# Bank pairs for the seven products, earlier weight sums, closer inverse units and longer first weight rows in a fused spectral-filter and gated-MLP kernel

## Chip, cores and metric

The kernel runs on one core of one Trainium2 chip. The metric is the device time in microseconds (us) of one execution; the median over several executions is compared.

## What is computed

```python
xn = layernorm(x)                        # x: (1, 2048, 512) bf16
X  = rfft2(xn, axes=(-2, -1))            # (1, 2048, 257) complex
y  = irfft2(X * (w_r + 1j * w_i), s=(2048, 512)).astype(bf16)
h  = gelu(xn @ w_gate) * (xn @ w_up)     # w_gate, w_up: (512, 1792)
out = x + y + h @ w_down                 # w_down: (1792, 512)
```

Two branches read the same normalised x: a spectral filter (a two-dimensional Fourier transform, a product with a weight per frequency, the transform back) and a gated MLP. Their results are added to x.

## The kernel before, in words

**Rows and blocks.** x lies in SBUF as `x_sb`, 16 tiles of 128 rows by 512; tile j is also where the result of these rows is summed up, and it is written out when all its parts are in. The MLP takes four tiles at a time: block b has the tiles 4b to 4b+3. `xnT` holds the normalised rows transposed.

**The MLP.** For each block and each of 14 chunks fc of 128 hidden columns, `gate` (line 842) and `up` (856) make four matmuls of 128x512 each into one PSUM bank. ScalarE takes gelu of the gate's bank into one of three `gl` buffers (854), and VectorE multiplies it with up's bank into `hT` (872). The down projection of two tiles, `down` (879), is 14 plain matmuls per tile. That of the other fourteen tiles is done two tiles at a time as seven products of half-size blocks in place of eight (`product`, 728): step 0 to 6 of product (b, p) makes seven 128x256 matmuls each, for the tiles jA = 4b+p and jB = jA+2. Some products need sums of blocks of w_down (`sums_T`, 717: T[0] to T[3], made once) and of h (`sum_01`, 692, and `sums_S`, 674). A product holds two PSUM banks, bx and by, over its seven steps: the steps use bx, bx, by, by, bx, by, by; after step 0 ScalarE copies bx to by (776), and after step 3 by to bx. VectorE adds finished parts to x_sb (`add_to`, 650) or stores them with x in `tw` (`base`, 778, for jA after step 2 and jB after step 3). From there until `release` (762), which comes for jB at step 5 and for jA at step 6, the tile is locked.

**The spectral branch.** It is cut into small units that are placed between the matmuls of the MLP. `butter` (419) folds xnT into `fold`; unit D (433) transforms along the columns, `units_A` (462) makes the first half of the transform along the rows, the result goes through DRAM (scr1) and comes back as `tv` (`load_tv`, 457). Unit B(g) and unit C(g), g = 0 to 7 (565, 588), make the second half and the first half of the transform back. Each takes two neighbouring banks, which ScalarE empties in one copy of 128x1024. Between B and C VectorE multiplies with the frequency weights (584), which are loaded in parts into a ring (`load_W`, 551; `keep_256`, 560, copies one column aside on POOL). C reads `cm`, a table loaded in four parts on POOL's queue. C's results go through DRAM (scr2) and come back as `vv` (612). The inverse units E(j) and F(j), j = 0 to 15 (618, 802), finish tile j: E is four matmuls, a ScalarE copy and a small POOL copy; F is four matmuls, a ScalarE copy and four VectorE additions (825 to 828), which leave the result in one of four `ys` buffers. `add_y` (831) then adds ys to x_sb[j] with an accumulating DMA on POOL's queue. If the tile is locked, it is put off until the release.
`mini` (491) does the same work for one left-over column.

**The order of the work.** Nothing is scheduled at run time. The Python program walks through the blocks and chunks, and `hook` (913) is called after each gate, each up and each product step (and three times in a down); it counts up, and before counting it emits whatever `at(h, ...)` has planned for this number. In the blocks 2 and 3 a turn is therefore three hooks: gate, up, product step. Block 2 starts at hook 69, block 3 at 111, product (2,0) comes just before the hooks 113, 116, ... 131, product (2,1) before 134, 137, ... 152, and the last two products (3,0) and (3,1) close the kernel with 14 steps. F(j)'s additions come right after F(j), and its add_y three hooks later. Every engine runs its own instructions in the order in which they were emitted; `op` (150) adds the semaphore waits, per tile key.

**PSUM banks.** `take(n, dur, ...)` (324) picks banks at build time by an estimate: it keeps a time pt of the work emitted so far and for each of the eight banks a time at which it should be free, and takes the n neighbouring banks whose latest time is the earliest. A product sets its banks to 1e9 until its last step.

**SBUF places.** `arena` has 8192 columns: the table `am` (0 to 3071), fold 0 (4096 to 6143) and fold 1 (6144 to 8191). T[0] to T[3], 1792 columns each, and a sum for products (0,p) use the same columns later. The last readers of fold 0 and fold 1 are the units D of tiles 8 to 11 (hooks 31 to 34) and 12 to 15 (hooks 39 to 42), that of am is units_A at hook 44. `cm` shares its columns with `ev1` and `xn`.

**Loads at the start.** SP's queue and ScalarE's queue each load one half (64 rows) of x tiles 0 and 1, then two chunks of a weight (w_up on SP, w_gate on ScalarE), the half of tiles 2 and 3, and two more chunks (352 to 357). A chunk is 128 columns, so that two chunks are rows of 512 bytes. SP's queue loads all that follows. The first six chunks of gate and up are first done for tiles 0 and 1 alone (1005 to 1023).

Of the kernel before, what the change touches and what calls it, by code (L numbers as in the profile page):

```python
# [214 lines left out]
def bass_parallel_sum__spectral_gfnet__glu_gated_geglu__prompt_kernel(  # L215
# [23 lines left out]
    wgv = B_w_gate.rearrange("(dc p) f -> p dc f", p=P)  # L239
    wuv = B_w_up.rearrange("(dc p) f -> p dc f", p=P)  # L240
    wdv = B_w_down.rearrange("(fc p) d -> p fc d", p=P)

    with ExitStack() as es:
        def sb(name, shape, dt):
            return es.enter_context(nc.sbuf_tensor(name, shape, dt))
# [6 lines left out]
        arena = sb("arena", [P, 8192], F16)  # L252
        am = arena[:, 0:3072].rearrange("p (j c) -> p j c", j=NJ)
        fold = [arena[:, 4096 + 2048 * i:6144 + 2048 * i].rearrange("p (a c) -> p a c", a=4) for i in range(2)]
        T = [arena[:, 1792 * k:1792 * k + 1792].rearrange("p (f c) -> p f c", f=7) for k in range(4)]
        AKEYS = ["am"] + [("fold", i, a) for i in range(2) for a in range(4)]
        wg_sb = sb("wg", [P, 4, FF], BF16)
        wu_sb = sb("wu", [P, 4, FF], BF16)
# [65 lines left out]
        def take(n, dur, hold=None, ops=1):  # L324
            i = min(range(9 - n), key=lambda i: max(free[i:i + n]))
            pt[0] += dur
            if hold is None:
                act_t[0] = max(act_t[0], pt[0] + 0.25) + 0.2 + 0.43 * n
                end = act_t[0]
            else:  # L330
                end = pt[0] + hold
            for k in range(i, i + n):
                free[k] = end
            return i

        def dma(eng, dst, src, r=(), w=()):
            return op(eng, lambda e: e.dma_start(dst, src), r=r, w=w, dma=True)  # L337
# [4 lines left out]
        def load_x(j0, n, b, eng):  # L342
            dma(eng, x_sb[64 * b:64 * b + 64, j0:j0 + n, :], xv[b, :, j0:j0 + n, :], w=[("x", j, b) for j in range(j0, j0 + n)])

        def load_w(t, v, nm, lo, hi, eng):
            cs = slice(P * lo, P * hi)
            dma(eng, t[:, :, cs], v[:, :, cs], w=[(nm, i) for i in range(lo, hi)])
# [4 lines left out]
        for b, eng, t, v, nm in ((0, "sp", wu_sb, wuv, "wu"), (1, "act", wg_sb, wgv, "wg")):  # L352
            load_x(0, 1, b, eng)
            load_x(1, 1, b, eng)
            load_w(t, v, nm, 0, 2, eng)
            load_x(2, 2, b, eng)
            load_w(t, v, nm, 2, 4, eng)
        op("act", lambda e: e.activation(warm_o[:], mhalf[:, 0:1], ACT.Gelu_apprx_tanh), r=["mhalf"], w=["warm_o"])
        load_w(wg_sb, wgv, "wg", 4, 6, "sp")
        load_w(wu_sb, wuv, "wu", 4, 6, "sp")  # L360
        load_x(4, 4, 0, "sp")
        load_x(4, 4, 1, "sp")
        dma("sp", fd[:], c_fd.ap(), w=["fd"])
# [243 lines left out]
        def readers(keys):  # L607
            return [ev for key in keys for ev in pr.readers.get(key, [])]
# [62 lines left out]
        def s_keys(b, k, f0, f1):  # L671
            return [("S", b, k, f) for f in range(f0, f1)]
# [35 lines left out]
        def s01(k, f0, f1):  # L708
            if k == 0:
                v = arena[:, 7168 + P * f0:7168 + P * f1]  # L710
            else:
                assert f1 <= 4 or f0 >= 4
                row = 2 * (k == 2) + (f0 >= 4)
                v = xb[:, 2048 * row + P * (f0 % 4):2048 * row + P * (f0 % 4) + P * (f1 - f0)]
            return v.rearrange("p (f c) -> p f c", c=P)

        def sums_T(k):
            B = lambda i, c: wd_sb[:, 7 * i:7 * i + 7, 256 * c:256 * c + 256]
            a, b2, r = ((B(0, 1), B(0, 0), []), (B(1, 1), T[0], [("T", 0)]), (B(1, 1), B(0, 1), []), (B(1, 0), T[1], [("T", 1)]))[k]
            op("dve", lambda e: e.tensor_tensor(T[k], a, b2, ALU.subtract), r=r + [("wd", fc) for fc in range(NFC)],  # L720
               w=[("T", k)], after=readers(AKEYS))

        wb = {}

# [3 lines left out]
        def product(b, p, step):  # L728

            jA, jB = 4 * b + p, 4 * b + p + 2  # L730
            cA, cB = slice(P * p, P * p + P), slice(256 + P * p, 256 + P * p + P)
            h = hT[b % 2]
            if step == 0:
                wb[p] = take(1, 0.0, 1e9), take(1, 0.0, 1e9)
            bx, by = wb[p]
            bk = (bx, bx, by, by, bx, by, by)[step]
            c0, c1 = slice(0, 256), slice(256, 512)
            if b < 2:
                SS = lambda k: (lambda f: s01(k, f, f + 1)[:, 0, :], [("s01", k)])
                for k in ((0, 1), (2,), (), (), (), (), ())[step]:  # L740
                    sum_01(b, p, k)
            else:
                SS = lambda k: (lambda f: ssum(b, k, f, f + 1)[:, 0, cA], s_keys(b, k, 0, 7))
            HH = lambda o, cs, t: (lambda f: h[:, f + o, cs], [("hT", b % 2, f + o, p + 2 * t) for f in range(7)])
            TT = lambda k: (lambda f: T[k][:, f, :], [("T", k)])
            BB = lambda o, cs: (lambda f: wd_sb[:, f + o, cs], [("wd", f + o) for f in range(7)])
            (st_, r1), (mv, r2) = ((HH(0, cA, 0), BB(0, c0)), (HH(7, cA, 0), BB(7, c0)), (SS(1), TT(1)), (SS(2), TT(2)),
                                   (HH(7, cB, 1), TT(3)), (SS(0), TT(0)), (SS(3), BB(7, c1)))[step]
            o = bank(bk)[:, 0:256]

            def fn(e):
                ins = None
                for f in range(7):
                    ins = e.matmul(o, st_(f), mv(f), start=(f == 0 and step in (0, 5)), stop=(f == 6), skip_group_check=True)  # L754
                return ins
            pt[0] += 0.77
            op("pe", fn, r=r1 + r2, w=[("ps", bk)])
            rk = [("ps", bk)]
            t12, t22 = tw[:, p, 0:256], tw[:, p, 256:512]
            last = b == 3  # L760

            def release(j):
                for f in locked.pop(j):
                    f()
                if last:
                    assert done[j] == 1
                    for bb, eng in ((0, "sp"), (1, "act")):
                        dma(eng, ov[bb, :, j, :], x_sb[64 * bb:64 * bb + 64, j, :], r=acc(j), w=[("out", j, bb)])
                else:
                    part_done(j)  # L770

            if b < 2 and step == 2:
                sum_01(b, p, 3)

            def copy(dst, src):
                return op("act", lambda e: e.activation(bank(dst)[:, 0:256], bank(src)[:, 0:256], ACT.Copy), r=[("ps", src)], w=[("ps", dst)], after=war(("ps", dst)))  # L776

            def base(t, j, *after):
                locked[j] = []
                op("dve", lambda e: e.tensor_tensor(t, o, x_sb[:, j, 256:512], ALU.add), r=rk + [("acc", j, 1), ("x", j, 0), ("x", j, 1)], w=[("tw", p, j == jA)],  # L780
                   after=war(("tw", p, j == jA)) + list(after))

            if step == 0:
                copy(by, bx)
            elif step == 1:
                add_to(jA, o, rk, 0)
            elif step == 2:
                base(t12, jA)
            elif step == 3:
                base(t22, jB, copy(bx, by))  # L790
            elif step == 4:
                add_to(jB, o, rk, 0)
            elif step == 5:
                add_to(jB, o, rk + [("tw", p, False)], 1, t22)
                release(jB)
            else:
                add_to(jA, o, rk + [("tw", p, True)], 1, t12)
                release(jA)
                free[bx] = free[by] = pt[0] + 1.2
            hook()  # L800
# [105 lines left out]
        def at(h, *calls):  # L906
            plan.setdefault(int(h), []).extend(calls)
# [19 lines left out]
                at(h0 + i // 2, t)  # L927
            at(89 + s // 2 if s > 3 else 47 + s, (keep_256, s))
        cmv = c_cm.ap().rearrange("p (h r c) -> p h r c", h=NJ, r=2)
        for i, h0 in enumerate((52, 57, 63, 68)):  # L930
            hs = slice(4 * i, 4 * i + 4)
            at(h0, (load_late, cm[:, hs], cmv[:, hs], [("cm", 2 * i), ("cm", 2 * i + 1)], (["ev1"], ["ev1", ("xn", 0)], [("xn", 1), ("xn", 2)], [("xn", 2), ("xn", 3)])[i]))
        at(60, (load_late, gm[:], c_g.ap().rearrange("p (a c) -> p a c", a=4), ["gm"]))
        for m in range(1, 4):
            a = (5, 15, 23)[m - 1]
            t = (16, 25, 33)[m - 1]
# [31 lines left out]
        for jg in range(4):  # L968
            at(99, (load_vv, jg))
        for j in range(NJ):  # L970
            at(107 + 2.6 * j, (unit_E, j))
            at(110.5 + 2.6 * j, (unit_F, j))
        for k in range(4):
            at(46 + k, (sums_T, k))
        for k in range(4):
            at((101, 101, 102, 103)[k], (sums_S, 2, 0, 4, (k,)))
            at((106, 106, 107, 107)[k], (sums_S, 2, 4, 6, (k,)))
# [122 lines left out]
```

## Time and profile before

| | |
|---|---|
| median of 5 runs | 187.98 us (186.61 to 191.28) |
| profiled execution, its own time | 186.61 us |
| its span (first to last instruction) | 184.8 us |
| granted TensorE clock | 1.00 in the whole span |
| gate and up matmuls (lines 851, 866), busy | 58.6 us each |
| DMA moved | 26.83 MB, 145 GB/s on average |

PE is TensorE's matmuls, PEld its weight loads, DVE VectorE, ACT ScalarE, POOL GpSimd, SP the engine that only issues DMAs. L754 is line 754 of the kernel. Matmuls are pipelined and their ends are modelled, so a busy PE is not PE at its peak. A line of waits gives the waiting instruction, what released it, the sum, how often and the longest. The chain of waits is followed back from the last instruction of the program.

### The profile page before, as it was taken

How to read it: one execution, taken by the hardware profiler on the slowest of the kernel's cores; microseconds unless marked ns; L12 is line 12 of the kernel's file. 1: busy time of each engine (PE TensorE's matmuls, PEld its weight loads, DVE VectorE, ACT ScalarE, POOL GpSimd, SP SyncE). 2: the span in 40 equal slices, each digit the busy share in tenths (PEclk: the TensorE clock that was granted, in tenths of full speed). 3: DMA queues.
4: the chain of work that ended last, by engine and by line, in shares of the span. 5: the costliest groups of instructions: out<-in, count | busy, mean ns of one | idle time of the engine just before them, and what ended most of it. 6: DMA issues, size and time to landing. Idle time of an engine off the chain costs nothing.

```text
span 184.8 us, 3814 instructions
## 1 busy us (share of the span) xinstructions
PE 175.8 (95%) x1417; PEld 107.9 (58%) x1417; DVE 130.6 (71%) x322; ACT 94.3 (51%) x157; POOL 53.8 (29%) x106
## 2 busy tenths in 40 slices
PE   7899999999999999989997999999999999899993
PEld 2478654555555454545653656556666676566882
DVE  3677899996442399647795468787875776689752
ACT  1344548676475442456664556435756766554110
POOL 2110263642316010356481000001334434434100
PEclk9999999999999999999999999999999999999999
DMA  4999998798989968255863112185145555344304
GB/s 115 285 255 311 335 278 301 201 175 173 181 134 207 120 147 121 70 167 136 220 177 88 57 57 60 58 242 216 28 82 100 103 105 109 63 73 67 79 0 114
DMA packets 27954, 26.83 MB, mean 145 GB/s; under 512 B 2992, under 2 KB 24880, under 8 KB 27808
## 3 DMA queue, kind: packets, MB, share of 16 engines
q1 hardware_dynamic: 21504, 18.04, 40.3%
q0 software_dynamic: 4272, 7.24, 18.8%
q10 hardware_dynamic: 2160, 1.31, 2.6%
q8 instruction: 11, 0.18, 0.4%
q14 instruction: 7, 0.06, 0.1%
HBM read 18.19 MB, written 6.29 MB: 132 GB/s over the span
## 4 chain that ended last, share of the span: by engine, by line
PE 69%; DVE 13%; DMA 6%; ACT 3%; issue 3%; SPq 2%; ACTq 1%; POOL 1%; DVEq 0%
PE ps L851 19%; PE ps L754 19%; PE ps L866 18%; DMA wu<-in_B_w_up_dram 4%; PE ps L887 3%; DVE hT L872 3%; DVE st L383 3%; SPq L337 2%; DMA x_sb<-tv 2%; PE ps L598 2%; DVE arena L720 2%; PE ps L626 2%; PE ps L809 2%; PE ps L573 1%; PE ps L405 1%
## 5 line engine op out<-in xcount | busy, mean ns | idle before, releaser
L851 PE MATMUL ps<-xnT,wg 128*128 128x512 f16 (+1 forms) x248 | 58.6, 359 | 0.6 <-ACT xnT L995 0.6
L866 PE MATMUL ps<-xnT,wu 128*128 128x512 f16 (+1 forms) x248 | 58.6, 359 | 0.2 <-DMA wu<-in_B_w_up_dram 0.2
L872 DVE TENSOR_TENSOR hT<-ps,gl 128x512 bf16<-128x512 f32 (+1 forms) x62 | 39.3, 636 | 20.3 <-PE ps L866 13.5
L854 ACT ACTIVATE gl<-ps 128x512 bf16<-128x512 f32 (+1 forms) x62 | 34.5, 556 | 32.3 <-PE ps L851 31.0
L866 PEld LDWEIGHTS ps<-xnT,wu 128*128 128x128 bf16 x248 | 23.4, 98 | 20.4 <-DMA wu<-in_B_w_up_dram 0.5
L851 PEld LDWEIGHTS ps<-xnT,wg 128*128 128x128 bf16 x248 | 22.9, 98 | 16.6 <-issue 2.1
L340 POOL DMA_DIRECT2D wring<-in_A_w_r_dram x32 | 18.5, 610 | 17.6 <-DVE early L584 7.5
L635 POOL COPY tv<-tv 1x128 bf16<-1x128 bf16 x16 | 4.7, 292 | 48.3 <-ACT tv L633 48.3
L835 POOL DMA_DIRECT2D x_sb<-tv x16 | 13.8, 862 | 4.7 <-DVE tv L828 4.5
L584 DVE TENSOR_TENSOR early<-early,wring 128x1024 bf16<-128x1024 f16 x16 | 10.3, 687 | 4.2 <-ACT early L579 4.2
L383 DVE BATCH_NORM_STATS2 st<-x_sb 128x6 f32<-128x512 bf16 x16 | 10.6, 681 | 3.0 <-DMA x_sb<-in_A_x_dram 3.0
L754 PE MATMUL ps<-wd,hT 128*128 128x256 bf16 x98 | 12.5, 273 | 0.0
L653 DVE TENSOR_TENSOR x_sb<-ps,x_sb 128x256 bf16<-128x256 f32 (+1 forms) x16 | 7.3, 454 | 7.1 <-PE ps L887 3.7
L450 ACT ACTIVATE early<-ps 128x512 f16<-128x512 f32 x16 | 9.5, 595 | 5.4 <-PE ps L446 5.4
L776 ACT ACTIVATE ps<-ps 128x256 f32<-128x256 f32 x14 | 5.2, 370 | 13.7 <-PE ps L754 13.7
L815 ACT ACTIVATE tv<-ps 128x512 bf16<-128x512 f32 x16 | 9.5, 595 | 4.8 <-PE ps L809 4.8
L633 ACT ACTIVATE tv<-ps 128x512 bf16<-128x512 f32 x16 | 9.5, 595 | 4.3 <-PE ps L626 4.3
L754 PE MATMUL ps<-arena,xnT 128*128 128x256 f16 x84 | 10.5, 273 | 0.5 <-DVE tw L780 0.5
L391 POOL TENSOR_TENSOR rstd<-vpe,mhalf 128x4 f32<-128x4 f32 (+1 forms) x5 | 4.5, 904 | 22.1 <-DVE vpe L390 22.1
L579 ACT ACTIVATE early<-ps 128x1024 f16<-128x1024 f32 x8 | 8.2, 1022 | 5.4 <-PE ps L573 5.4
L754 PEld LDWEIGHTS ps<-wd,hT 128*128 128x128 bf16 x98 | 9.3, 98 | 2.3 <-issue 0.2
L482 ACT ACTIVATE early<-ps 128x1024 f16<-128x1024 f32 x8 | 7.9, 1022 | 4.6 <-PE ps L477 3.8
(104 smaller groups left out, 242.9 us busy)
## 6 DMA issues: line engine op xcount, KB each, us to landing
wring<-in_A_w_r_dram POOLq DMA_DIRECT2D x32, 64.2 KB, 3.6
wring<-in_A_w_i_dram SPq DMA_DIRECT2D x32, 64.2 KB, 3.7
tv<-scr SPq DMA_DIRECT2D x8, 256.0 KB, 5.8
scr<-early SPq DMA_DIRECT2D x8, 256.0 KB, 2.2
wring<-scr SPq DMA_DIRECT2D x4, 512.0 KB, 7.1
x_sb<-tv POOLq DMA_DIRECT2D x16, 128.0 KB, 2.7
scr<-early SPq DMA_DIRECT2D x14, 128.0 KB, 3.8
out_dram<-x_sb SPq DMA_DIRECT2D x28, 64.0 KB, 2.1
```

Of the source, the lines that this page charges most:

```text
L340: op(eng, lambda e: e.dma_start(dst, src), w=list(keys) + list(also), dma=True, after=[("pe", pr.cnt["pe"])])
L383: op("dve", lambda e: e.bn_stats(st[:, j, :], x_sb[:, j, :]), r=[("x", j, 0), ("x", j, 1)], w=[("st", j)])
L450: op("act", lambda e: e.activation(x4.rearrange("p (a c r) -> p a c r", a=2, r=4), bank(bk).rearrange("p (a r c) -> p a c r", a=2, r=4), A ...
L584: op("dve", lambda e, k=k: e.tensor_tensor(pp[i][k], xc[i], W[k][g % 4][:, :, :, 0:256], ALU.mult), r=[("xc", i)] + [key for c in range(2) ...
L633: op("act", lambda e: e.activation(z, bank(bk).rearrange("p (a c) -> p a c", a=4), ACT.Copy, scale=SC_E), r=[("ps", bk)], w=[zk] + (TVK if ...
L754: ins = e.matmul(o, st_(f), mv(f), start=(f == 0 and step in (0, 5)), stop=(f == 6), skip_group_check=True)
L815: op("act", lambda e: e.activation(o2, bank(bk), ACT.Copy), r=[("ps", bk)], w=[ok] + (TVK if j < 2 else []))
L835: op("pool", lambda e: e.dma_start(x_sb[:, j, :], ys, accum_op=ALU.add), r=[yk + (0,), yk + (1,), ("x", j, 0), ("x", j, 1)] + acc(j), w=ac ...
L851: ins = e.matmul(bank(bg)[:, 0:n], wg_sb[:, dc, fc * P:(fc + 1) * P], xnT[:, dc, c0:c0 + n], start=(dc == 0), stop=(dc == 3))
L854: op("act", lambda e: e.activation(gl[k % 3][:, 0:n], bank(bg)[:, 0:n], ACT.Gelu_apprx_tanh), r=[("ps", bg)], w=[("gl", k % 3)])
L866: ins = e.matmul(bank(bu)[:, 0:n], wu_sb[:, dc, fc * P:(fc + 1) * P], xnT[:, dc, c0:c0 + n], start=(dc == 0), stop=(dc == 3))
L872: op("dve", lambda e: e.tensor_tensor(hT[b % 2][:, fc, h0:h0 + n], bank(bu)[:, 0:n], gl[k % 3][:, 0:n], ALU.mult), r=[("ps", bu), ("gl", k ...
```

## The change

Five edits.

- The four places for T in arena are dealt out in another order (T[0] in the columns from 3584, T[1] from 5376, T[2] from 0, T[3] from 1792), each waits only for the readers of what lies there, and `sums_T` is emitted at the hooks 41, 43, 47 and 52 in place of 46 to 49.
- A product takes its two banks in one `take(2)`, so they are neighbours.
- The first weight loads bring three chunks each (rows of 768 bytes), and the two SP loads of chunks 4 and 5 are gone.
- The first part of `cm` is loaded at hook 45 in place of 52.
- The inverse units come every 2.2 hooks in place of 2.6.

```diff
-        T = [arena[:, 1792 * k:1792 * k + 1792].rearrange("p (f c) -> p f c", f=7) for k in range(4)]
+        T = [arena[:, 1792 * k:1792 * k + 1792].rearrange("p (f c) -> p f c", f=7) for k in (2, 3, 0, 1)]
...
             load_x(1, 1, b, eng)
-            load_w(t, v, nm, 0, 2, eng)
+            load_w(t, v, nm, 0, 3, eng)
             load_x(2, 2, b, eng)
-            load_w(t, v, nm, 2, 4, eng)
+            load_w(t, v, nm, 3, 6, eng)
         op("act", lambda e: e.activation(warm_o[:], mhalf[:, 0:1], ACT.Gelu_apprx_tanh), r=["mhalf"], w=["warm_o"])
-        load_w(wg_sb, wgv, "wg", 4, 6, "sp")
-        load_w(wu_sb, wuv, "wu", 4, 6, "sp")
...
-               w=[("T", k)], after=readers(AKEYS))
+               w=[("T", k)],
+               after=readers([("fold", i, a) for i in range(k + 1) for a in range(4)] if k < 2 else ["am"]))
...
             if step == 0:
-                wb[p] = take(1, 0.0, 1e9), take(1, 0.0, 1e9)
+                i = take(2, 0.0, 1e9)
+                wb[p] = i, i + 1
...
-        for i, h0 in enumerate((52, 57, 63, 68)):
+        for i, h0 in enumerate((45, 57, 63, 68)):
...
         for j in range(NJ):
-            at(107 + 2.6 * j, (unit_E, j))
-            at(110.5 + 2.6 * j, (unit_F, j))
+            at(107 + 2.2 * j, (unit_E, j))
+            at(110.5 + 2.2 * j, (unit_F, j))
         for k in range(4):
-            at(46 + k, (sums_T, k))
+            at((41, 43, 47, 52)[k], (sums_T, k))
```

## The prediction, made before the result was known

> **What bounds the kernel now.** I read busy times first, then TensorE's waits, then the chain of waits.
>
> ```profile
> PE 175.8 (95%) x1417; PEld 107.9 (58%) x1417; DVE 130.6 (71%) x322; ACT 94.3 (51%) x157; POOL 53.8 (29%) x106
> ```
>
> TensorE is in use nearly all the time and the change removes no matmul, so only time in which TensorE stands can be won. The waits of the PE engine alone (us in total, times, longest) say how little that is:
>
> ```profile
> PE ps L754 <- DVE tw L780: 1.4, 2, 0.9
> PE ps L598 <- ACT early L579: 1.2, 1, 1.2
> ...
> PE ps L598 <- ACT gl L854: 0.4, 1, 0.4
> ...
> PE ps L516 <- ACT early L579: 0.2, 1, 0.2
> PE ps L866 <- DMA wu<-in_B_w_up_dram: 0.2, 1, 0.2
> ```
>
> Matmul ends are modelled, so I measure a stall from start to start: a 128x512 matmul holds the next back 0.216 us, a 128x256 one 0.109. By that the stalls are: 0.34 us at 12.21 (wu load), 0.69 at 74.35, about 1.2 at 79.2 to 80.8, 1.29 at 101.15, 1.05 at 161.41. The chain of waits (start us, us, what) shows what precedes three of them:
>
> ```profile
> 65.55 0.60 DVE hT L872
> 66.15 2.08 DVE arena L720 x2
> 68.24 0.60 DVE hT L872
> 68.84 1.00 DVE arena L720
> ...
> 73.88 0.43 DVE tw L780
> 74.35 0.94 PE ps L754 x7
> ...
> 99.59 0.37 PE ps L573 x8
> 99.98 1.03 ACT early L579
> 101.15 0.63 PE ps L598 x16
> ...
> 154.75 3.62 DMA x_sb<-tv
> 158.80 0.68 DVE xnT L689
> ...
> 161.01 0.34 DVE tw L780
> 161.41 0.94 PE ps L754 x7
> ```
>
> First, VectorE is full from 64.3 to 74.3 with the weight sums (L720) among its work, and `base` (L780) is late. Second, a unit C stands until ScalarE has copied out unit B just before it. Third, an accumulating DMA into x_sb holds VectorE back.
>
> **What the Trainium skill says.** "PSUM — Partial Sum Buffer", PSUM bank collisions: TensorE must not write a bank that another engine reads, so accesses are guarded by bank. The trace agrees: C at 101.15 starts only after the 1.02 us copy of B from 99.98. "DMA: Bandwidth & Descriptors", Why small descriptors are slow: each packet bears a fixed overhead, so longer rows move more. The trace agrees: in the first 12.5 us a 512 B packet took 29 ns in the middle, a 1024 B one 46, that is 17.7 against 22.3 B/ns. "Trainium Kernel Development and Optimization", Key Constraints: queues issued from different engines share the same 16 DMA engines; a second queue saves issue time only. Page and trace agree: the DMA share is about 1.1 from 4.6 to 18.5 us.
>
> **Bank pairs.** I worked the planner's rule (line 325) through from its state at hook 71. Product (0,1) gets banks 5 and 6 as before, so nothing changes up to there, and the 1.2 us at 79.2 to 80.8 stay: C(0) takes bank 0 from a gate whose gelu ends at 79.73, and mini(1) takes B(1)'s pair. Product (1,0) held 6 and 0, which left the pairs 1-2 to 4-5; at hook 82 B(5) and C(4) both got 1-2. With 0 and 1 held, B(5) gets 5-6 and C(4) 2-3: banks last used by an up whose multiply starts at 97.30 and a gate whose gelu ends at 99.36. B(5) starts at 99.52 and needs 0.34, so C(4) goes at 99.86 instead of 101.15: 1.29 saved. C(3) no longer takes a bank from a late up: 0.55 becomes the usual 0.44, 0.1 saved. What follows C(4) is TensorE's own work. Later products draw pairs that the plan has free at least 1.0 us ahead. **-1.4.** No instruction is added.
>
> **Weight sums.** T(0) and T(1) (1.05 and 1.08 us) go from hooks 46 and 47 to 41 and 43, where VectorE is busy 1.38 of 4.62 us (55.4 to 60.1). T(1) waits for unit D(15), whose last matmul is at 58.24; queued behind it is the add of a down product at 62.65, so nothing is late. Some 2.1 us leave the full stretch; T(2) and T(3) keep clear of each other. `base` at 73.88 can be 2 us earlier, the last up ends at 73.66, and the 0.69 us go. But B(0), now at 75.22, would start at 74.53, and its last tv load lands at 74.45 by the trace. So the gain is between 0 and 0.69; I take **-0.5**, because of the next edit.
>
> **First part of cm to hook 45.** POOL issues it at about 62.5 instead of 69.11: it waits for TensorE there, and the six w copies now at 59.37 queue behind it by some 3 us. Their readers come after 95 us, and the W loads that need them at 78. Its 192 KB leave the tv loads' time (68.2 to 74.5, DMA share 0.87) and enter that of the scr1 writes (62.3 to 68.1, share 1.00): 128 rows of 1536 B, 8 on each engine at 111 ns, at most 0.9 us either way. Its reader C(0), at 79.87, has it landed 5 us early as it is. **0**, from -0.4 to +0.4.
>
> **First weight loads.** Two SP issues (0.51 us each) go; bytes are the same. In front of x's third part each queue now has 384 KB instead of 256, 256 KB more in all. At the 267 KB/us that both queues moved from 4 to 8 us it is 1.0 us; at about 37 ns for 768 B (between 29 and 46) the 768 KB gain 0.4 us back. So x's third part, landed at 8.17, lands at 8.6 to 9.1; its statistics on VectorE (the first multiply queues behind them), POOL's rstd and the normalisation follow in order, and the transposes now at 12.65, with 0.3 us in hand, start at 12.7 to 13.2. The stall of 0.34 at 12.21 goes, but gate 3, due at 10.55, may wait up to 0.6 for wg chunk 3 to 5. wg chunk 0 landed at 6.40 and is due at 7.91, wu at 6.86 for 8.35: about 0.9 later still fits. **+0.1**, from -0.34 to +0.8.
>
> **Inverse units at 2.2 hooks.** E, F, four VectorE additions, a POOL copy and an accumulating DMA, sixteen times as before, only closer: the last F at hook 143, not 149. What counts is `add_y(9)`, three hooks after F(9). Product (2,1) first adds to x row 9 at hook 137. Before, add_y(9) was at 136: issued 154.75, landed 158.37, and VectorE stood 2.13 us until 158.46. Now it is at 133. From E(12) in that hook to the end of the product step TensorE needs 2x0.87+2x0.77+4x0.22 = 4.2 us; POOL issues 1.6 us after an E, as now (153.17 to 154.75), and lands 2.7 to 3.6 us later, so VectorE waits 0.1 to 1.0 instead of 3. Row 11 goes at 137 against 143 (142 before), and wins its 0.55 wait. The others are clear, rows 8 and 10 included (131, 135; product (2,0) lets go at 131 and 128). Does VectorE carry it? Per turn (gate, up, product: three hooks): multiply 0.69, product add 0.36, 1.36 times four additions of 0.285 is 1.55, together 2.6 of 3.1 us. From hook 132 to 143 the block-3 sums join: six F give 6.8, four multiplies 2.7, four sums 2.7, three adds 1.3, 13.5 us against TensorE's 4x2.5+10x0.22 = 12.2. It falls 1.3 us behind, and `base` has 1.74 us of gate and up before TensorE needs it. After hook 143 it has 2.0 of 2.5 us and catches up. Bank slack stays near 2 us. So the 1.05 goes, up to 0.3 may come back: **-1.0**.
>
> **Sum.** -1.4 -0.5 +0 +0.1 -1.0 = -2.8. The profiled execution took 186.61 (span 184.8), so 183.8. It was the fastest of five; from the median 187.98 I go to **185.2**. The tail is unchanged: TensorE runs through the last 14 steps, then the output DMA.
>
> **Rivals.**
> *A part is given back (0.20).* The start loses 0.8 instead of 0.1, tv lands late and takes the 0.5: -2.8+0.7+0.5 = -1.6, 186.4. For it: a saturated start, 0.08 us between B(0) and its load. Against it: longer rows move faster.
> *All comes and a little more (0.10).* -0.34 at the start, -0.69 for T and 0.4 from earlier tv: 183.9 or so.
> *Slower (0.10).* One mechanism: the accumulating DMAs can't keep the closer pace. F(j+4) writes the ys buffer of F(j) 8.8 hooks later, 5.8 after add_y(j), which is about 6.6 us; where issue and landing take longer, VectorE stands in unit F's additions, and every multiply waits behind them. At the old 3.0 us a row against 2.6, ten rows cost 4 us; with the 1.05 kept too, 187.98-1.8+4 = 190.2. Against it: DMAs issued at 140.11 and 141.48 landed 0.57 apart, at 144.54 and 145.11, so more than the pace needs gets through.
> The banks' part not doing what it says is excluded only after hook 71; before, it does nothing, as counted.
>
> **How the numbers follow.** My forecast has 0.60, with a range of its own of 184.2 to 186.1. A measurement here can tell about 1%, 1.88 us. Faster by more: nearly all of 0.60, the 0.10, and a third of the 0.20: 0.73. Within 1%: 0.18. Slower: 0.09. The range 183.5 to 187.5 leaves out most of the slow case and little below.
>
> **What would show it.** Right: no wait of L598 on L579 near 98; L754 no more waiting on L780; no VectorE wait on x_sb<-tv over 1 us; waits at C(0) and mini(1) as before. Wrong: a new TensorE wait on wg at 10 to 12 us, on tv at B(0), or VectorE additions (L825) waiting for DMAs from 130 us on.

## The result, and the profile after

The median is 185.94 us (184.64 to 191.37, 27 executions) against 188.09 us of the kernel before measured beside it (186.02 to 191.44, 48 executions). The ratio of the compared executions is 0.9887, with a 95% interval of 0.9863 to 0.9911. That is 1.13% or 2.1 us less. Some executions of either kernel are 2 to 6 us longer than the rest, those of the changed kernel mostly with a lower granted TensorE clock for a while; the ratios here leave such executions out, the medians do not.

The profile after is of the changed kernel in an execution of 186.63 us with a span of 184.8 us and the clock at 1.00. Busy time by engine, first part of the page:

```profile
PE 174.6 (94%) x1417; PEld 108.2 (59%) x1417; DVE 130.6 (71%) x322; ACT 94.3 (51%) x157; POOL 53.5 (29%) x106
```

The same 1417 matmuls, and the same work on all engines. As before, only TensorE's standing time could change. TensorE's waits in the changed kernel (us in total, times, longest; its lines 571 and 596 are units B and C, 573 and 598 before; 577 is ScalarE's copy behind B, 579 before; 986 is the first transposes):

```profile
PE ps L571 <- DMA tv<-scr: 2.1, 1, 2.1
PE ps L986 <- DVE cmx L393: 1.3, 1, 1.3
...
PE ps L866 <- DMA wu<-in_B_w_up_dram: 0.9, 1, 0.9
...
PE ps L596 <- ACT gl L854: 0.4, 1, 0.4
...
PE ps L514 <- ACT early L577: 0.2, 1, 0.2
```

The two largest waits of before, L754 on L780 and L598 on L579, have no successor in the list. The waits of C(0) and of `mini` are there as before. In their place stands a new first line: unit B(0) waits for the load of tv. The chain of waits (start us, us, what) shows what leads there, and what has become of the other two places:

```profile
63.44 0.68 ACTq L337
64.24 1.03 ACT early L480
65.30 5.84 DMA scr<-early
71.21 0.31 SPq L337
71.56 6.14 DMA tv<-scr
77.84 0.41 PE ps L571 x8
...
102.09 0.34 PE ps L571 x8
102.43 0.44 PE ps L596 x16
...
159.56 0.77 PE ps L754 x7
160.55 0.86 PE ps L851 x4
```

Before, the chain came to B(0) through VectorE's weight sums. Now it comes through two DMAs of 5.84 and 6.14 us, a write to DRAM and the read back. Unit C(4) follows B(5) with nothing between them: by the starts of their matmuls B(5) begins at 102.02 and C(4) at 102.26. From 102 us on the chain is TensorE's own work; the stall at 161 is gone.

Start to start, TensorE's stalls in the two traces compare as follows (us, beyond the least distance for the shape of the matmul in front; for C(4) beyond the 0.10 us that the change from B to C takes where nothing waits):

| place | before | after |
|---|---|---|
| first gate begins at | 7.91 | 8.24 |
| an up of the first chunks, on the wu load | 0.34 | 1.02 |
| product (0,1), step 3, on `base` behind the weight sums | 0.69 | none |
| B(0), on tv | none | 2.31 |
| C(4), on B(5)'s banks | 1.39 | none |
| product (2,1), step 3, on `base` | 1.05 | none |

3.13 us went and 3.32 us came (0.33, 0.68 and 2.31). The two spans are equal (184.8 us), but the trace of before is of the fastest of its five executions, and that of after is of one longer than the median of its kernel (186.63 against 186.14). Two traces show where stalls lie; the gain can be read only from the medians and ratios. The experiments divide it.

### The profile page after: what moved, and what is told of

The parts are those of the page before. It is cut to its first block, busy times and chain, and to the rows that moved or that the text cites. A ratio compares the mean times of both kernels' runs of the same rounds, so it can differ in the third digit from the quotient of the medians.

```text
span 185.9 us, 3824 instructions
## 1 busy us (share of the span) xinstructions
PE 176.4 (95%) x1417; PEld 109.2 (59%) x1417; DVE 131.0 (70%) x322; ACT 94.3 (51%) x157; POOL 54.5 (29%) x106
## 4 chain that ended last, share of the span: by engine, by line
PE 75%; DMA 8%; DVE 8%; ACT 3%; issue 2%; POOL 1%; SPq 0%; ACTq 0%; DVEq 0%
PE ps L851 21%; PE ps L866 21%; PE ps L754 19%; DMA tv<-scr 3%; DMA scr<-early 3%; DVE st L381 3%; PE ps L887 3%; DMA x_sb<-in_A_x_dram 2%; PE ps L624 2%; PE ps L809 2%; PE ps L596 2%; DVE hT L872 1%; PE ps L571 1%; PE ps L403 1%; ACT early L480 1%
## 5 line engine op out<-in xcount | busy, mean ns | idle before, releaser
L851 PE MATMUL ps<-xnT,wg 128*128 128x512 f16 (+1 forms) x248 | 59.5, 363 | 0.6 <-ACT xnT L995 0.6
L866 PE MATMUL ps<-xnT,wu 128*128 128x512 f16 (+1 forms) x248 | 59.4, 363 | 0.0
L633 POOL COPY tv<-tv 1x128 bf16<-1x128 bf16 x16 | 5.2, 325 | 42.3 <-ACT tv L631 42.3
L835 POOL DMA_DIRECT2D x_sb<-tv x16 | 13.1, 865 | 2.8 <-DVE tv L828 2.5
L754 PE MATMUL ps<-wd,hT 128*128 128x256 bf16 x98 | 12.5, 273 | 0.0
L754 PEld LDWEIGHTS ps<-wd,hT 128*128 128x128 bf16 x98 | 9.3, 98 | 2.3 <-issue 0.2
L754 PE MATMUL ps<-arena,xnT 128*128 128x256 f16 x84 | 10.5, 273 | 0.0
```

The lines of the kernel that those rows point to most:

```text
L835: op("pool", lambda e: e.dma_start(x_sb[:, j, :], ys, accum_op=ALU.add), r=[yk + (0,), yk + (1,), ("x", j, 0), ("x", j, 1)] + acc(j), w=ac ...
L851: ins = e.matmul(bank(bg)[:, 0:n], wg_sb[:, dc, fc * P:(fc + 1) * P], xnT[:, dc, c0:c0 + n], start=(dc == 0), stop=(dc == 3))
L866: ins = e.matmul(bank(bu)[:, 0:n], wu_sb[:, dc, fc * P:(fc + 1) * P], xnT[:, dc, c0:c0 + n], start=(dc == 0), stop=(dc == 3))
```

## Experiments

Where a gain in us is given, it is the ratio less one, times the median of before measured beside it (188.03, 188.27 or 187.69 us). The theories are set out with the expectations.

**The change once more, and one edit taken back at a time.** First the changed kernel unaltered (after_again):

> The changed kernel once more, beside the kernel before. Expected ratio about 0.988. Theory 1 (the first weight loads hold x back): its profile shows the second half of x tile 1 landing near 5 us and not at 4.1, and the first gate at 8.5 to 9.0. Theory 2 (the late x was an accident of one execution): the first gate is at 7.9 as before, and only the wait of unit B(0) for the tv load remains, 1 to 2 us.

Measured: 0.9864 [0.9835, 0.9893], 2.6 us less than before. It repeats the result. Its trace is the one shown above, with B(0)'s wait of 2.31 us. It agrees with neither theory on the start: the second half of x tile 1 landed at 4.46 us and the first gate began at 8.24, between the two.

u_rows has the changed kernel with the first loads of before:

```diff
-            load_w(t, v, nm, 0, 3, eng)
+            load_w(t, v, nm, 0, 2, eng)
...
-            load_w(t, v, nm, 3, 6, eng)
+            load_w(t, v, nm, 2, 4, eng)
+        load_w(wg_sb, wgv, "wg", 4, 6, "sp")
+        load_w(wu_sb, wuv, "wu", 4, 6, "sp")
```

> The changed kernel with the first weight loads put back to two chunks each. Theory 1 (the longer first loads hold x back): 0.5 to 1 us faster than the changed kernel, ratio to before 0.983 to 0.986. Theory 2 (the longer rows are about neutral): same as the changed kernel, ratio 0.987 to 0.990. If longer rows help: 0.990 to 0.993.

Measured: 0.989 [0.9845, 0.9935], the same as with the longer rows. In its trace B(0) waited only 0.84 us for tv, and a gate 0.48 us for wg. The span was 182.5 us, the shortest of all traces, but its median ratio did not follow. That the longer rows cost a large part of what was missing is not supported.

u_cm puts the first part of `cm` back to hook 52:

```diff
-        for i, h0 in enumerate((45, 57, 63, 68)):
+        for i, h0 in enumerate((52, 57, 63, 68)):
```

> The changed kernel with the first part of cm back at hook 52. Theory P (the 192 KB of cm among the scr1 writes make B(0)'s tv load late): B(0) waits at most 0.7 us for tv and the kernel is about 1 us faster, ratio to before 0.982 to 0.985. Theory Q (the tv load is late whatever is beside it, since TensorE is now ready earlier and the transfers are at their limit): B(0) waits as long or longer, ratio 0.987 to 0.991.

Measured: 0.9887 [0.9807, 0.9967]. B(0) waited 2.42 us for tv, so the wait does not need the move of cm. Here cm was issued at 70.29, just ahead of the tv loads at 70.50 and 70.85; the second of these landed at 77.85, after 7.0 us.

u_units puts the inverse units back to every 2.6 hooks:

```diff
-            at(107 + 2.2 * j, (unit_E, j))
-            at(110.5 + 2.2 * j, (unit_F, j))
+            at(107 + 2.6 * j, (unit_E, j))
+            at(110.5 + 2.6 * j, (unit_F, j))
```

> The changed kernel with the inverse units back at 2.6 hooks. By the prediction the wait for the accumulating DMA of row 9 comes back: a VectorE wait for x_sb<-tv of about 2 us, a stall of L754 on L780 of about 0.9 us near 158, and the kernel 1.0 us slower than the changed one, ratio to before 0.992 to 0.995. Rival (the closer units only move the load): same as the changed kernel, 0.987 to 0.990.

There is no ratio for it, so the size is not shown this way. The trace answers the question of mechanism. TensorE's waits and VectorE's waits in u_units (us in total, times, longest):

```profile
PE ps L754 <- DVE tw L780: 0.9, 1, 0.9
```

```profile
DVE x_sb L651 <- DMA x_sb<-tv: 2.1, 1, 2.1
```

Both lines of before are back when only this edit is taken out: VectorE stands 2.1 us for the accumulating DMA, `base` is late, and step 3 of product (2,1), which writes the bank that `base` reads, starts 1.05 us late, at 161.21.

**One edit done alone.** In the kernel before, only the longer first rows (only_rows):

> The kernel before with the three-chunk first weight loads alone. Theory (the longer first loads hold back x tile 1 and the chunks 3 to 5): first gate 0.3 to 1 us later than before, a wait of TensorE for wu or wg of about 1 us near 12, in some executions a lower granted TensorE clock near 10 us because TensorE stood over 1.5 us after its warm-up; ratio 1.003 to 1.008. Rival (rows are neutral, as predicted +0.1): 0.998 to 1.002.

Measured: 1.002 [0.999, 1.0049], +0.4 us (-0.2 to +0.9). TensorE's waits on the first weights in it:

```profile
PE ps L850 <- DMA wg<-in_B_w_gate_dram: 0.3, 1, 0.3
...
PE ps L865 <- DMA wu<-in_B_w_up_dram: 0.2, 1, 0.2
```

The waits stay small but do not go: chunks 3 to 5 of wg landed at 11.03 and of wu at 11.85 us, which is when they are needed. The first gate began at 7.93 (before: 7.91), so it was not held back in this trace. One part of the theory came true, and the ratio does not contain it: 7 of 22 executions had a mean granted clock of 0.991 or less, against 1 of 33 of the kernel before beside them, and the medians over all executions are 189.59 and 188.27 us. Over all kernels here whose clock is on record it is 29 of 90 executions with three-chunk loads and 9 of 119 with two-chunk loads. Why the one goes with the other is not shown.

Only the two neighbouring banks (only_banks):

```diff
-                wb[p] = take(1, 0.0, 1e9), take(1, 0.0, 1e9)
+                i = take(2, 0.0, 1e9)
+                wb[p] = i, i + 1
```

> The kernel before with the bank pairs alone. Prediction: the stall of C(4) near 101 goes, 1.3 us, ratio 0.991 to 0.995. Rival (what is won there is lost to a later wait): 0.998 to 1.001, and the profile shows a new stall between 102 and 160.

Measured: 0.9906 [0.9873, 0.9938], -1.8 us (-2.4 to -1.2). Its waits (line 756 is the product, 782 `base`, 598 unit C, 856 gelu):

```profile
PE ps L756 <- DVE tw L782: 1.4, 2, 0.8
...
PE ps L598 <- ACT gl L856: 0.4, 1, 0.4
```

The wait of unit C on the copy of unit B is gone. Both waits on `base` stay, and so does C(0)'s. The 1.39 us at C(4) are gone, and 0.09 us at C(3).

Only the inverse units at 2.2 hooks (only_units):

> The kernel before with the inverse units at 2.2 hooks alone. Prediction: the stall of 1.05 us at 161 goes, ratio 0.993 to 0.997, no VectorE wait for x_sb<-tv over 1 us. Rival (VectorE falls behind between hooks 132 and 143): a stall of L754 on L780 stays, ratio 0.998 to 1.003.

Measured: 0.9929 [0.9895, 0.9964], -1.3 us (-2.0 to -0.7). Its waits are the complement (755 is the product, 781 `base`, 598 and 579 unit C and the copy):

```profile
PE ps L598 <- ACT early L579: 1.2, 1, 1.2
...
PE ps L755 <- DVE tw L781: 0.5, 1, 0.5
```

Of the two waits on `base`, 1.4 us together before, the one at 161 us is gone and the one at 75 stays.

Only the weight sums, with their new places in arena (only_sums):

```diff
-... for k in range(4)]
+... for k in (2, 3, 0, 1)]
...
-               w=[("T", k)], after=readers(AKEYS))
+               w=[("T", k)],
+               after=readers([("fold", i, a) for i in range(k + 1) for a in range(4)] if k < 2 else ["am"]))
...
-            at(46 + k, (sums_T, k))
+            at((41, 43, 47, 52)[k], (sums_T, k))
```

> The kernel before with the weight sums in their new places and hooks alone. Prediction taken apart: L754 no longer waits for L780 near 75, 0.69 us, and B(0) then stands at its tv load. Theory S (tv lands 12.2 to 12.8 us after the first scr1 write is issued, whatever TensorE does): B(0) waits 0 to 0.8 us and the ratio is 0.998 to 1.002. Rival (the full 0.69 us is won): 0.995 to 0.997, no wait for tv.

Measured: 1.0032 [0.9979, 1.0085], +0.6 us (-0.4 to +1.6). TensorE's waits and the chain in it (line 573 is unit B):

```profile
PE ps L755 <- DVE tw L781: 1.3, 1, 1.3
...
PE ps L573 <- DMA tv<-scr: 0.7, 1, 0.7
```

```profile
64.59 4.41 DMA scr<-early
...
69.43 6.14 DMA tv<-scr
...
75.71 0.41 PE ps L573 x8
```

One wait on `base` is left, that at 162 us. The stall of 0.69 us ahead of step 3 of product (0,1) is gone. B(0) waits 0.88 us start to start for tv instead. What the edit frees, the load takes.

**Banks and units together** (banks_units: the two diffs of only_banks and only_units, nothing else):

> The kernel before with the bank pairs and the inverse units at 2.2 hooks, and nothing else. If the two gains simply add (0.9906 times 0.9929): ratio 0.981 to 0.986, faster than the whole change. If one takes from the other: 0.987 to 0.990.

Measured: 0.9844 [0.9781, 0.9906], -2.9 us. The product of the two single ratios is 0.9906 x 0.9929 = 0.9836, so the gains add. That it beats the whole change (0.9887 and 0.9864) is not shown; the intervals overlap. This kernel has neither the sums, nor the rows, nor cm moved, and yet B(0) waited 1.93 us for tv in its trace, start to start, on top of the 0.69 us stall:

```profile
PE ps L573 <- DMA tv<-scr: 1.8, 1, 1.8
```

**Can the wait for tv be moved away?** w3late is u_rows with the loads of the fourth weight part moved from beside the DRAM writes to after them:

```diff
-        for s, h0 in enumerate((20, 27, 34, 40, 61, 66, 70, 75)):
+        for s, h0 in enumerate((20, 27, 34, 49, 61, 66, 70, 75)):
...
-            at(89 + s // 2 if s > 3 else 47 + s, (keep_256, s))
+            at(89 + s // 2 if s > 3 else (47, 48, 49, 60)[s], (keep_256, s))
```

> The changed kernel with two-chunk first loads again, and the eight frequency-weight loads of s=3 moved from the hooks 40 to 43 to 49 to 52, behind the last tv load. Theory R (the tv load of block 3 is late because scr1 and tv queue behind 512 KB of weights): scr1 lands within 3.5 us, tv lands before B(0) is due, B(0) waits at most 0.3 us, and the kernel is 1 us or more faster than the changed one, ratio 0.975 to 0.982. Rival S (the tv transfer itself, 16 partitions, is slow whatever else runs): B(0) still waits 0.7 us or more, ratio 0.984 to 0.990.

Measured: 0.9841 [0.9808, 0.9873]; that of u_rows overlaps it. Its wait for tv:

```profile
PE ps L573 <- DMA tv<-scr: 1.5, 1, 1.5
```

Start to start B(0) still waited 1.66 us. Half of theory R is borne out: the first two DRAM writes landed 2.5 and 2.8 us after their issue, against 3.9 to 5.5 in all other traces. The other half is not: the last write landed at 68.79, and the second tv load, issued at 69.21, landed only at 76.40, after 7.2 us. Four of the weight loads had gone out on POOL's queue from 67.09 to 68.73, so not behind the tv loads but ahead of them. So this run doesn't test what happens with nothing beside either.

cm56 is u_rows with the first part of `cm` after the tv loads:

```diff
-        for i, h0 in enumerate((45, 57, 63, 68)):
+        for i, h0 in enumerate((56, 57, 63, 68)):
```

> The changed kernel with two-chunk first loads and the first part of cm at hook 56, behind the last tv load and in nobody's way. Theory P (cm beside scr1 or tv makes tv late): tv lands at most 12.5 us after the first scr1 issue, B(0) waits at most 0.3 us, ratio 0.978 to 0.984. Theory S (the scr1 writes and the tv load need that long by themselves): B(0) waits 0.6 us or more, ratio 0.984 to 0.989.

Measured: 0.9846 [0.9797, 0.9896]; at 184.69 us its median is the lowest of all kernels, but its interval overlaps those of the change and of banks_units, so it is not shown to be better than they are. The chain of waits:

```profile
65.45 5.29 DMA scr<-early
...
71.17 6.04 DMA tv<-scr
...
77.34 0.41 PE ps L573 x8
```

cm was issued only at 73.66, 2.5 us after the second tv load, and no weights lay beside that load (the last of them landed at 68.18, beside the writes). The tv load took 6.04 us all the same, and B(0) waited 1.66 us.

**More warm-up matmuls.** warm17 is the changed kernel with 17 warm-up matmuls in place of 13, to fill TensorE's wait before the first gate:

```diff
-        warm(13)
+        warm(17)
```

> The changed kernel, all five edits, with 17 warm-up matmuls in place of 13. They end near 7.1 us and not near 6.3, so that TensorE stands less before the first transposes. Theory (the lower granted clock of some executions comes from that stand): no execution has a mean granted clock of 0.991 or less, where 8 of 28 of the changed kernel had; ratio near 0.987. Rival (the clock falls for another reason): as often as before.

Measured: 1.0072 [1.0009, 1.0135], 190.18 us in the median; two of the four executions in this ratio had the lower clock. The first of TensorE's waits, and the row of the granted clock (tenths, 40 slices of 4.72 us):

```profile
PE ps L851 <- DMA wg<-in_B_w_gate_dram: 4.0, 1, 4.0
```

```profile
PEclk9996999999999999999999999999999999999999
```

The theory that the lower clock is only a matter of the short stand behind the warm-up falls: that stand was filled (the wait of L986 is 0.2 us here, 1.3 above), and yet 4 of 6 executions had a mean clock of 0.991 or less, against 6 of 22 of after_again and 7 of 28 in the first measurement of the changed kernel (the expectation counts 8). What the trace shows is a gate that stood 4.0 us, to 15.03, for wg chunks 3 to 5, and the clock at 6 tenths in the slice around the end of this stand (14.2 to 18.9 us). Why the load was late in this kernel is not settled by one trace.

## Why the prediction came out as it did

The forecast was 185.2 us, a gain of 2.8 us. The measured median of 185.94 is 0.7 us above it and inside its range. The sum by its terms:

| term | predicted | measured alone |
|---|---|---|
| bank pairs | -1.4 | -1.8 (-2.4 to -1.2) |
| weight sums | -0.5 | +0.6 (-0.4 to +1.6) |
| first part of cm | 0 | not done alone; moved back or later, no difference that the intervals show |
| first weight loads | +0.1 | +0.4 (-0.2 to +0.9) |
| inverse units | -1.0 | -1.3 (-2.0 to -0.7) |
| whole | -2.8 | -2.1 (-2.6 to -1.7) |

The four single ratios multiply to 1.002 x 0.9906 x 0.9929 x 1.0032 = 0.9887, which is the ratio of the whole. By their intervals the product is known to about 0.8% only, so the exact agreement is chance; within that the parts neither help nor hinder each other. That the forecast came so near is in part luck too: two terms won a little more than forecast and two less.

**Bank pairs: right.** The pairs followed from the planner's rule, and the places came out as worked out: C(4) follows B(5) at once, C(0) and `mini` wait as before. The size is on the low side, within the interval; from B(5)'s start to C(4)'s it takes 0.24 us and not the 0.34 of the prediction.

**Inverse units: right.** The chain from add_y to VectorE's add to `base` to step 3 of product (2,1) was the one. In the changed kernel the accumulating DMAs of 152.62 and 154.46 landed at 155.24 and 156.91, and the add at 158.29 had nothing to wait for. Before, one issued at 154.75 landed at 158.37 and held it. The predicted remainder of up to 1.0 us on VectorE did not appear there; in warm17 it was 0.7 us. The rival in which the accumulating DMAs can't keep the closer pace did not happen: no wait of L825 on a DMA is among VectorE's waits.

**Weight sums: the term that failed.** The prediction priced the stall at 0.69 us, saw that B(0) could not begin before tv's landing at 74.45, 0.08 us ahead of the then earliest start, and still took 0.5. It treated that landing as a fixed date. It is not: the trip from the first DRAM write's issue to tv's last landing was 12.15 us in the one trace shown then, and from 12.65 to 14.61 us in the later ones. TensorE's own work beside it, without stalls, is the start of B(0) less its wait, from the same issue:

| kernel | DRAM trip | B(0)'s wait | start of B(0), from the first write | less the wait |
|---|---|---|---|---|
| before | 12.15 | 0 | 12.92 | 12.23 (less the 0.69 stall) |
| only_sums | 12.83 | 0.88 | 12.97 | 12.09 |
| u_rows | 12.80 | 0.84 | 12.94 | 12.10 |
| cm56 | 13.61 | 1.66 | 13.75 | 12.09 |
| u_units | 13.74 | 1.79 | 13.88 | 12.09 |
| after_again | 14.26 | 2.31 | 14.40 | 12.09 |
| u_cm | 14.37 | 2.42 | 14.51 | 12.09 |

TensorE needs 12.1 us in each of these traces; the trip needs at least as long. The late sums mostly filled time that would have been a wait anyway, and taking them out of the way uncovers it. An estimate from the traces of the five kernels without this edit: B(0) could have started at 12.09 us, or 0.14 us after its load where that is later, which would have won 0.6 us in the trace of before and 0 to 0.1 us in the other four. The prediction's own list named this as a sign of being wrong: a new wait on tv at B(0).

What makes the trip 12.15 us once and 14.6 another time is settled in part. Up to B(0), before, only_banks, only_units and banks_units emit the same instructions in the same order with the same waits, and their trips were 12.15, 12.76, 12.65 and 14.61 us. So no edit is needed for the difference; it comes about between executions of the same instructions. The places of cm and of the weight loads, each moved by itself, did not bring the wait below 1.6 us. The writes of 128 KB took 3.7 to 5.8 us, in w3late 2.5 to 4.2, and the second tv load 5.9 us or more.

Side by side the fourteen traces show two things behind this. In thirteen of them six or seven weight loads were still under way when the first DRAM write was issued, and this write landed 0.2 to 0.3 us after the last of them, 3.9 to 5.1 us after its own issue; in w3late none was, and it took 2.5. And the second tv load took 5.9 to 6.1 us in the eleven traces in which no other load was issued shortly ahead of the tv loads, but 7.0 to 7.2 us in the three in which POOL's queue had just been given one: weights in w3late, cm in u_cm and banks_units. With cm at hook 52 this is a race: in all seven such traces cm is issued 6.81 us after the first write, and the first tv load when the writes have landed, 5.88 to 7.06 us after it. Both are read off traces, one for each kernel; w3late is a test of the first, the second has none. A kernel with the weights and cm both behind the tv loads was not run, and how often each length comes is open.

**First part of cm: not shown apart.** Beside the writes, at hook 45, the second pair of writes landed 2.1 to 2.6 us after the first (w3late aside), elsewhere 1.2 to 2.1, which fits the bound of 0.9 us, though the two ranges touch. The prediction did not see that cm at hook 52 can get ahead of the tv loads. The DMA shares it names, 0.87 and 1.00, belong to the slices 69.3 to 73.9 and 60.1 to 64.7; in the stretches it names the shares are 0.77 and 0.81. The term does not rest on them.

**First weight loads: within its bounds, the sign not shown.** The interval holds zero. A 768-byte packet took 36 ns in the middle in after_again, where the estimate was 37. x's third part landed at 8.20 and 9.21 us in after_again, against a forecast of 8.6 to 9.1 for the later of the two. The prediction had the wait on wu going; it grew to 1.02 us there. But with the loads of before it was no steadier: in u_rows, banks_units, cm56 and only_sums a wait on wg stood in its place, 0.5 to 1.6 us. In these traces the late one is on the queue whose first weight load was issued second (2.26 to 2.27 us against 1.98 to 2.00; in u_rows both at 2.01), and which queue that is changes between executions of the same loads. The lower clock that goes with these loads (above, at only_rows) is in no term of the prediction.

**Of the rivals,** the one in which a part is given back came closest: 186.4 us, with tv late as its reason, against 185.94 measured. The larger banks and units made up in part for the sums that gave nothing. The terms of the rival in which all comes add to -3.8, which is 184.1 us and not 183.9.

## What to carry to other kernels

Before a stall is priced as a gain, ask what the stalled instruction's successors wait for, and take that other date with its scatter, not from one trace: here a stall of 0.69 us with a DMA landing close behind was worth, by the estimate above, 0.6 us in one trace and next to nothing in four others. Buffers that are held long are worth holding side by side where others need neighbours (0.9% here), and the effect can be worked out at the desk from the allocator's rule. When edits touch different stages, do each alone: here the product of four single ratios met the whole within their intervals, and two of the four brought no gain that shows.

## What the runs showed of the hardware

A round trip through DRAM takes longer than its bytes alone would at the rate seen elsewhere. In cm56 the two tv loads, 512 KB together, were issued from 70.82 and landed by 77.21, which is 80 KB/us, although nothing else was under way until 73.66. At the start of the kernel, between 4 and 8 us, two queues together moved 267 KB/us.

Two queues issued alike are not served alike. In after_again the ScalarE queue's wg chunks 3 to 5, issued at 3.19, landed at 10.96, and SP's wu chunks, issued at 3.46, landed at 12.42. In warm17 SP's landed at 10.99 (issued at 3.19) and ScalarE's, issued 0.29 us later, only at 14.98, behind two x loads that SP had issued after it (landed 12.03 and 13.43).

The Trainium skill, "TensorE: Matmul & The Clock Gate", section The HAM clock gate, says that the clock halves after an idle window of about 3.4 us, and that the windows run free of the kernel. warm17 agrees: after the stand of 4.0 us the granted clock is one half from 15.23 to 18.64, and gate and up of four matmuls began 0.85 to 0.86 us apart from 15.69 to 18.25, against 0.43 to 0.44 us before the stand and later. Another execution of the changed kernel, of 187.72 us, agrees less well: the clock is one half from 8.84 to 12.26, and gate and up went at 0.8 to 0.85 us from the first gate at 9.04, though the warm-up had ended only at 6.25, 2.6 us before the clock fell, and TensorE had done 0.63 us of transposes before that gate. The length of the gap from warm-up to first gate does not decide it: it was 2.79 us there, and 2.84 us in banks_units with the same transposes inside, where the clock stayed full. What does decide is not shown.
